# Stores of prepared weights ordered four steps behind the making of their low part, and an inverse square root spread over more steps

## The chip, the cores and the metric

The kernel runs on one core of a Trainium2 chip. Its time is device microseconds (us) for one execution. The kernel before took 1690.93 us (median of 3 runs, 1688.75 to 1692.35). One execution was profiled; its trace gives the rows below.

## The reference

Three layers, one behind the other, all with float32 results:

```python
# attention without softmax: batch 8, 8 heads, 576 positions, head size 64
kv  = einsum('bhsd,bhse->bhde', k, v)
out = einsum('bhsd,bhde->bhse', q, kv)
x   = out / sqrt(mean(out * out, -1) + 1e-6) * g_norm      # -> [4608, 512]
# layer 1, 512 -> 1536 -> 512
xn  = x / sqrt(mean(x * x, -1) + 1e-6) * rms_g
x   = (silu(xn @ w_gate) * (xn @ w_val)) @ w_out
# layer 2, 512 -> 2048 -> 512
h   = maximum(x @ w_in, 0)
out = (h * h) @ w_out2
```

The weights come as 64-bit floats.

## The kernel before, in words

**Tiling.** The 4608 rows are nine blocks of 512. They go through TensorE in stages: layer 1 on blocks 0 and 1 (stage 0), on block 2 (stage 1), then on pairs of blocks, then layer 2 in the same way. Every number that is multiplied is the sum of a high part (what TensorE's fast float32 form keeps) and a low part (the rest); a product takes three passes, high by high, low weight by high, high by low. Pairs of blocks, from stage 2 on, use a scheme of seven block products instead of eight, which needs sums and differences of quarters of the weights.

**Tick.** Six matmuls of 128x512 are one product, called here a product or a tick. After each, `tick()` advances the counter `now[0]` and emits what is due: work put off by `after`, the attention of the coming blocks (`chain`), and steps of the preparation of weights (`prep_step`). All instructions stand in the order in which the Python code emits them (a manual schedule); each engine works its own list off in that order, and SP (the queue that issues every DMA) too. A wait at the head of a list holds everything behind it.

**Preparation of a unit.** A unit is a 128x1024 piece of a weight matrix, named by letter and number (g0, v0, g1, v1, ... for gate and value, o for the first output matrix, i and p for layer 2). Its steps have fixed times: load (L131), three steps that turn 64-bit floats into 32-bit ones (`bits_1` on ScalarE, L139; `bits_2` and `bits_3` on VectorE, L143, L144, L150), the high part (`hi`, ScalarE, L180), the low part (`lo`, VectorE, L183), and a store of both to DRAM (`put`, SP, L192). Units of kind "all" then make the second half, the sums for the seven products, and have a second `hi`, `lo` and `put`. Steps of all units wait in one queue, `prep_q`, in the order of their times. `prep_step(False)`, which `tick` calls, leaves the step at the head of the queue for later while its `landed` says no. Where a weight is wanted that is not ready, `w_direct` (stage 0) and `w_fetch` (later stages) take steps from the queue at once, without asking `landed`.

**Weights in stage 0.** While weights are still being made, the products read the prepared tiles `ws` directly, g0 in products 0 to 3, v0 in 4 to 7, g1 in 8 to 11, v1 in 12 to 15, g2 in 16 to 19, v2 in 20 to 23. The high part is read by a product's first two matmuls, the low part by the next two. From stage 1 on a tile `wt` is fetched from DRAM into a ring of five. Fetching begins near the end of stage 0, and only when `prep_q` is empty:

```python
                    if first[0] and nb == 1 and n >= len(seq) - 3 and not prep_q:
                        streams[0] = True
```

**Attention.** For each block of 512 rows: four times an `o_mm` (TensorE), then `att_g` (L433, VectorE), squares on ScalarE (L442, L446) that overwrite the bank, and sums (L451); then at step u `att_m`, at u+1 the inverse square root by three Newton rounds (`att_r`, L470 to L481), at u+2 and u+3 the four products `att_y` (L493), and from u+9 the transposes (`x1_T`, L500, TensorE), which read all four. Block 1 (the `direct` one) has shorter times and is transposed into SBUF in stage 0 (`x_hi` L521, `x_lo` L525).

**What frees TensorE's banks.** In stages with seven products VectorE adds (L686) an accumulator to a copy; the product that writes this bank next waits for the addition.

Of the kernel before, what the change touches and what calls it, by code (L numbers as in the profile page):

```python
# [11 lines left out]
F32 = mybir.dt.float32  # L12
# [23 lines left out]
W_RING = 5  # L36
N_SUMS = 5
LAND = 6


@with_exitstack
def attn_moe_moe(
# [14 lines left out]
    nc = tc.nc  # L57
# [50 lines left out]
    def prep_unit(key, kind, raws, plains, outs, ahead=7):  # L108

        m, f = key  # L110
        src, place = w_src[m]
        pair, e = pair_of(key)
        if pair not in wd:
            wd[pair] = [dram.tile([128, 4, 2, 2, 256], F32, name=f"wd_{m}{f}_{h}") for h in range(2)]
        st = {}

        def plain_tile():

            at = next(plains)
            if len(at) == 2:  # L120
                t = at[0].tile([128, 2, 2, 512], F32, tag=at[1], name="wpl")
                st["s"], st["w"] = t[:, 0], t[:, 1]
            else:
                st["s"] = at[0].tile([128, 2, 512], F32, tag=at[1], name="wps")
                st["w"] = at[2].tile([128, 2, 512], F32, tag=at[3], name="wpw")

        def load():
            pool, tag = next(raws)
            st["t"] = now[0]
            st["r"] = pool.tile([128, 2, 512, 2], I32, tag=tag, name="wraw")  # L130
            nc.sync.dma_start(  # L131
                out=st["r"].rearrange("p u n w -> p (u n w)"), in_=src[f].rearrange("p u n -> p (u n)").bitcast(I32)
            )

        def bits_1():
            plain_tile()
            nc.scalar.activation(out=st["s"], in_=st["r"][:, :, :, 1].bitcast(F32), func=AF.Copy, scale=2.0**-112)  # L139

        def bits_2():
            hf, w = st["s"].bitcast(I32), st["w"].bitcast(I32)
            nc.vector.tensor_scalar(out=w, in0=hf, scalar1=-(2**31), scalar2=None, op0=ALU.bitwise_and)  # L143
            nc.vector.scalar_tensor_tensor(  # L144
                out=w, in0=st.pop("r")[:, :, :, 0], scalar=29, in1=w, op0=ALU.logical_shift_right, op1=ALU.bitwise_or
            )

        def bits_3():
            hf, w = st["s"].bitcast(I32), st["w"].bitcast(I32)
            nc.vector.scalar_tensor_tensor(  # L150
                out=w, in0=hf, scalar=3, in1=w, op0=ALU.logical_shift_left, op1=ALU.bitwise_or
            )

        def words_in():
            plain_tile()
            st["t"] = now[0]
            nc.sync.dma_start(out=st["w"], in_=wfd[key])

        def words_out():
            wfd[key] = dram.tile([128, 2, 512], F32, name=f"wf_{m}{f}")  # L160
            nc.sync.dma_start(out=wfd[key], in_=st["w"])

        def quarters(x):
            return x.rearrange("p u (h n) -> p (u h) n", h=2)

        def op(b, x, y, alu):
            of = {b: quarters(st["w"])[:, i] for b, (_, i) in place.items()}
            of |= {b: quarters(st["s"])[:, i] for b, (_, i) in PLACE_S.items()}
            nc.vector.tensor_tensor(out=of[b], in0=of[x], in1=of[y], op=alu)

        def hi(h):
            outs.rotate(-1)
            pool, tag = outs[-1]
            st["tag", h] = tag
            if kind in ("blocks", "words"):
                in_use[tag_of((pool, tag))] = key
            if pool is hop:
                hop_n[0] += 1
            st[h] = pool.tile([128, 4, 2, 256], F32R, tag=tag, name="ws")
            nc.scalar.activation(out=st[h][:, :, 0, :], in_=quarters(st["sw"[1 - h]]), func=AF.Copy)  # L180

        def lo(h):
            nc.vector.tensor_tensor(  # L183
                out=st[h][:, :, 1, :],
                in0=quarters(st["sw"[1 - h]]),
                in1=st[h][:, :, 0, :].bitcast(F32),
                op=ALU.subtract,
            )
            direct[key, h] = st[h]

        def put(h):
            nc.sync.dma_start(out=wd[pair][h][:, :, e], in_=st.pop(h).bitcast(F32))  # L192
            if not first[0] or h:
                put_at[st["tag", h]] = now[0]
            prepped.add((key, h))

        def sums():
            op("S1", "21", "22", ALU.add)
            op("S3", "11", "21", ALU.subtract)

        def hi_0():
            hi(0)

        def hi_1():
            hi(1)

        def sums_1():
            sums()

        def late(t):  # L210
            return now[0] - t >= LAND

        hi_0.ready = lambda: tag_of(outs[0]) not in in_use
        hi_0.landed = hi_1.landed = lambda: late(put_at.get(outs[0][1], -LAND))
        bits_1.landed = lambda: first[0] or late(st["t"])
        if kind == "sums":
            sums_1.landed = lambda: late(st["t"])
        head = [(-ahead, load), (-1 if kind == "all" else 1, bits_1), (2, bits_2), (3, bits_3), (4, hi_0), (5, lambda: lo(0))]
        tail = [
            (5, sums_1),  # L220
            (6, lambda: op("S2", "S1", "11", ALU.subtract)),
            (7, lambda: op("S4", "12", "S2", ALU.subtract)),
            (9, hi_1),
            (10, lambda: lo(1)),
            (13, lambda: put(1)),
        ]
        if kind == "all":
            return head + [(10, lambda: put(0))] + tail
        if kind == "blocks":
            return head + [(10, lambda: put(0))]  # L230
        if kind == "words":
            return head + [(8, words_out), (10, lambda: put(0))]
        return [(-2, words_in)] + tail

    in_use, put_at, hop_n = {}, {}, [0]
# [226 lines left out]
        nc.vector.tensor_scalar(out=z, in0=z, scalar1=1.0 / DM, scalar2=EPS, op0=ALU.mult, op1=ALU.add)  # L462
        m_t[j] = m

    def att_r(j):

        m = m_t.pop(j)
        a = small.tile([128, NS + NQ], F32, tag="a", name="a")
        r = small.tile([128, NS + NQ], F32, tag="r", name="r")
        nc.vector.tensor_scalar(  # L470
            out=a.bitcast(I32), in0=m.bitcast(I32), scalar1=1, scalar2=None, op0=ALU.logical_shift_right
        )
        nc.vector.tensor_scalar(
            out=r.bitcast(I32), in0=a.bitcast(I32), scalar1=-1, scalar2=MAGIC, op0=ALU.mult, op1=ALU.add
        )
        for _ in range(3):
            nc.vector.scalar_tensor_tensor(out=a, in0=r, scalar=-0.5, in1=r, op0=ALU.mult, op1=ALU.mult)
            nc.vector.tensor_tensor(out=a, in0=a, in1=m, op=ALU.mult)
            nc.vector.scalar_tensor_tensor(out=r, in0=a, scalar=1.5, in1=r, op0=ALU.add, op1=ALU.mult)
        rc = r[:, :NS].rearrange("p (c h) -> p c h", h=H)  # L480
        nc.vector.tensor_tensor(  # L481
            out=rc,
            in0=rc,
            in1=r[:, NS:].rearrange("p (c o) -> p c o", o=1).to_broadcast([128, NQ, H]),
            op=ALU.mult,
        )
        r_t[j] = r
# [54 lines left out]
    def o_events(j, t, gap, first_t, t_gap, direct=False):  # L542

        for c in range(NQ):
            i, u = j * NQ + c, t + gap * c
            if not direct:
                at(u, lambda i=i: (o_mm(i), q_load()))
            elif c:
                at(u, lambda i=i, c=c: (o_mm(i), q_load() if c == 1 else None))
            at(u + 1, lambda i=i: att_g(i))  # L550
            s = u if direct else u + 1
            at(s + 1, lambda i=i: att_sq(i))
            at(s + 2, lambda i=i: att_sum(i, 0))
            at(s + 3 - direct, lambda i=i: att_sg(i))
            at(s + 4 - direct, lambda i=i: att_sum(i, 1))
        u = t + gap * (NQ - 1) + (4 if direct else 6)
        at(u, lambda: att_m(j))
        at(u + 1, lambda: att_r(j))
        for c in range(NQ):
            at(u + 2 + c // 2, lambda c=c: att_y(j, c, nc.vector))  # L560
        for c in range(KC):
            v = first_t + t_gap * c
            if direct:
                at(v, lambda c=c: x1_T(j, c, tag="AB"[c % 2]))
                at(v + 1, lambda c=c: (x_hi(j, c), x_lo(j, c)))
            else:
                at(v, lambda c=c: x1_T(j, c))
                at(v + 1, lambda c=c: x1_out(j, c))
# [63 lines left out]
    def at(t, fn):  # L632
        seq_n[0] += 1
        insort(chain, (t, seq_n[0], fn))
# [370 lines left out]
    with tc.manual_schedule():  # L1005
# [68 lines left out]
        idle = psum.tile([128, 512], F32, tag="b5", name="idle")  # L1074
        keep(8)
        att_m(0)
        att_r(0)
        for c in range(NQ):
            att_y(0, c, nc.vector)
        prep_step()  # L1080
# [95 lines left out]
```

## Time and profile before

| what | before |
|---|---|
| median of 3 runs (lowest, highest) | 1690.93 us (1688.75, 1692.35) |
| the profiled execution | 1691.47 us, its span 1689.7 us |
| TensorE (PE) busy | 1656.5 us, 98% of the span |
| VectorE (DVE) busy | 1099.0 us, 65% |
| ScalarE (ACT) busy | 665.3 us, 39% |
| DMA of queue q1 | 441.54 MB, 77.1% of 16 engines' span |
| mean granted TensorE clock | 0.992 |

PE is TensorE's matmuls, PEld its weight loads. A row of the timeline gives start, length, engine, line, operation, tiles, and in brackets the idle time ahead of it with what ended it. The DMA's landing is the time at which the last of its data has arrived.

### The profile page before, as it was taken

To read this page: it belongs to the slowest core of one execution; us is meant where nothing else is said; L and a number is where in the kernel's file an instruction comes from. 1 tells how busy PE (TensorE), PEld (TensorE's weight loads), DVE (VectorE), ACT (ScalarE), POOL (GpSimd) and SP (SyncE) were. 2 spreads that over 40 slices of the span, in tenths; PEclk is the share of its full clock that TensorE was granted. 3 is DMA by queue.
4 is the path that set the end of the run, shared out by engine and by line. 5 is a ranking of instruction groups with operands and counts; after the bars stand their busy time and mean duration, and the time that the engine had idled before them with its cause. 6 is when DMAs were issued, how large, how long until landed. Compare 5 with 4: busy or idle time off the path is not lost.

```text
span 1689.7 us, 21279 instructions
## 1 busy us (share of the span) xinstructions
PE 1656.5 (98%) x8060; PEld 1361.2 (81%) x8060; DVE 1099.0 (65%) x1500; ACT 665.3 (39%) x908; POOL 0.7 (0%) x6
## 2 busy tenths in 40 slices
PE   8899999999999999999999999999999999999998
PEld 7688888788888887878888888878887887888887
DVE  6866685766885669653985347864884587468431
ACT  4332443244444444442543323533353345335331
POOL 0000000000000000000000000000000000000000
PEclk8999999999999999999999999999999999999999
DMA  9875689998998898787998866767676657766674
GB/s 327 270 285 222 235 279 350 367 341 291 374 319 279 272 334 312 263 316 248 347 356 281 280 212 194 239 200 217 195 241 201 212 193 238 212 206 217 194 226 142
DMA packets 146725, 442.89 MB, mean 262 GB/s; under 512 B 14016, under 2 KB 14016, under 8 KB 142272
## 3 DMA queue, kind: packets, MB, share of 16 engines
q1 hardware_dynamic: 146624, 441.54, 77.1%
q8 instruction: 64, 1.05, 0.2%
q14 instruction: 37, 0.30, 0.0%
HBM read 343.97 MB, written 97.52 MB: 261 GB/s over the span
## 4 chain that ended last, share of the span: by engine, by line
PE 82%; DVE 9%; DMA 6%; ACT 2%; issue 1%; SPq 0%; DVEq 0%; ACTq 0%
PE c L671 46%; PE acc L891 17%; PE a L926 9%; PE e L926 3%; PE d L926 3%; DVE ho L578 2%; PE ops L416 1%; DMA wt<-wd_o 1%; DMA wd_p<-ws 1%; DVE xo L578 1%; PE kvps L376 1%; PE ot L983 1%; DMA wt<-wd_g 1%; DVE ws L183 1%; DMA kvraw<-in_k_dram 1%
## 5 line engine op out<-in xcount | busy, mean ns | idle before, releaser
L671 PE MATMUL c<-xo,wt 128*128 128x512 f32 x3336 | 782.1, 392 | 6.7 <-DVE hr L686 4.2
L671 PEld LDWEIGHTS c<-xo,wt 128*128 128x128 f32 x3336 | 621.3, 188 | 136.8 <-DVE hr L686 5.5
L578 DVE TENSOR_TENSOR ho<-hr,ho 128x1024 fp32r<-128x1024 f32 x174 | 212.4, 1222 | 121.9 <-ACT ho L577 121.9
L891 PE MATMUL acc<-ho,wt 128*128 128x512 f32 x1200 | 278.4, 392 | 3.5 <-DMA wt<-wd_o 3.5
L891 PEld LDWEIGHTS acc<-ho,wt 128*128 128x128 f32 x1200 | 225.3, 189 | 51.7 <-DMA wt<-wd_o 4.7
L577 ACT ACTIVATE ho<-hr 128x1024 fp32r<-128x1024 f32 x174 | 183.7, 1058 | 171.8 <-PE acc L891 63.6
L686 DVE TENSOR_TENSOR c<-c,s 128x512 f32<-128x512 f32 x150 | 103.3, 688 | 163.2 <-PE c L671 155.7
L682 ACT ACTIVATE s<-c 128x512 f32<-128x512 f32 x204 | 120.9, 596 | 165.0 <-PE c L671 164.2
L926 PE MATMUL a<-ho,wt 128*128 128x512 f32 x768 | 178.7, 390 | 2.5 <-DVE ho L578 2.5
L926 PEld LDWEIGHTS a<-ho,wt 128*128 128x128 f32 x768 | 143.4, 188 | 35.2 <-DVE ho L578 5.6
L671 PE MATMUL c<-xo,ws 128*128 128x512 f32 x576 | 141.7, 400 | 7.9 <-ACT ws L180 4.9
L671 PEld LDWEIGHTS c<-xo,ws 128*128 128x128 f32 x576 | 107.1, 190 | 32.8 <-ACT ws L180 5.7
L686 DVE TENSOR_TENSOR hr<-c,s 128x512 f32<-128x512 f32 x54 | 37.1, 687 | 82.7 <-PE c L671 81.9
L926 PE MATMUL e<-ho,wt 128*128 128x512 f32 x384 | 88.3, 389 | 0.0
L743 DVE TENSOR_TENSOR hr<-c,hr 128x512 f32<-128x512 f32 x108 | 73.9, 686 | 19.0 <-PE c L671 17.5
L926 PEld LDWEIGHTS e<-ho,wt 128*128 128x128 f32 x384 | 72.1, 188 | 15.0
L738 ACT ACTIVATE r<-c 128x512 f32<-128x512 f32 x48 | 28.7, 598 | 137.0 <-PE c L671 137.0
L581 DVE TENSOR_TENSOR hr<-hr 128x1024 f32<-128x1024 f32 x64 | 78.2, 1222 | 1.1
L691 ACT ACTIVATE sg<-hr 128x512 f32<-128x512 f32 x54 | 34.1, 632 | 111.1 <-DVE hr L686 111.1
L578 DVE TENSOR_TENSOR xo<-xr,xo 128x1024 fp32r<-128x1024 f32 x53 | 64.2, 1219 | 16.4 <-ACT xo L577 16.2
L739 DVE TENSOR_TENSOR hr<-c,r 128x512 f32<-128x512 f32 x48 | 33.2, 692 | 61.2 <-ACT r L738 61.1
L691 ACT ACTIVATE sg<-c 128x512 f32<-128x512 f32 x54 | 32.1, 595 | 99.8 <-PE c L671 99.6
(79 smaller groups left out, 1281.7 us busy)
## 6 DMA issues: line engine op xcount, KB each, us to landing
wt<-wd_g SPq DMA_DIRECT2D x150, 512.0 KB, 6.4
wt<-wd_i SPq DMA_DIRECT2D x128, 512.0 KB, 4.1
wt<-wd_p SPq DMA_DIRECT2D x128, 512.0 KB, 4.7
wt<-wd_o SPq DMA_DIRECT2D x84, 512.0 KB, 4.5
wd_g<-ws SPq DMA_DIRECT2D x24, 1024.0 KB, 9.5
wd_i<-ws SPq DMA_DIRECT2D x16, 1024.0 KB, 7.6
wd_p<-ws SPq DMA_DIRECT2D x16, 1024.0 KB, 8.0
wraw<-in_wo_dram SPq DMA_DIRECT2D x14, 1024.0 KB, 7.5
```

Source lines behind the costliest of these rows:

```text
L577: nc.scalar.activation(out=dst[:, 0], in_=src, func=AF.Copy)
L578: eng.tensor_tensor(out=dst[:, 1], in0=src, in1=dst[:, 0].bitcast(F32), op=ALU.subtract)
L581: eng.tensor_tensor(out=o, in0=x, in1=y, op=ALU.subtract)
L671: nc.tensor.matmul(ps, lhsT=w[:, a, kc * 128:(kc + 1) * 128], rhs=x[:, b, kc, :], start=(start and n == 0 and kc == 0), stop=(n == 2 and k ...
L682: nc.scalar.activation(out=t, in_=ps, func=AF.Copy)
L686: nc.vector.tensor_tensor(out=o, in0=ps, in1=t, op=ALU.add)
L691: nc.scalar.activation(out=sg, in_=c, func=AF.Sigmoid)
L738: nc.scalar.activation(out=t, in_=c, func=AF.Relu)
L739: after(1, lambda: nc.vector.tensor_tensor(out=hr, in0=c, in1=t, op=ALU.mult))
L743: after(2, lambda: nc.vector.tensor_tensor(out=hr, in0=c, in1=hr, op=ALU.mult))
L891: nc.tensor.matmul(acc[c], lhsT=wt[:, a, (c % 2) * 128:(c % 2 + 1) * 128], rhs=x[:, b, e, :], start=(n == 0 and e == 0 and a + b == 0), st ...
L926: nc.tensor.matmul(ps, lhsT=w[e][:, a, d * 128:(d + 1) * 128], rhs=x[:, b, e, :], start=(i in (1, 2, 5) and q == 0 and e == 0 and a + b == 0),
```

## The change

The store of a half gets a `landed` of its own: it stays in the queue until four ticks after that half's low part was emitted. As `prep_q` is one queue, the steps behind it stay too. The root of a block that is not `direct` is emitted in three ticks (u+1, u+2, u+3), and its four products in the four ticks u+4 to u+7 instead of two each at u+2 and u+3. The transposes stay at u+9. No arithmetic is added or taken away.

```diff
+MADE = 4
@@ prep_unit
                 op=ALU.subtract,
             )
+            st["lo", h] = now[0]
             direct[key, h] = st[h]
...
+        def put_0():
+            put(0)
+
+        def put_1():
+            put(1)
+
+        put_0.landed = lambda: now[0] - st["lo", 0] >= MADE
+        put_1.landed = lambda: now[0] - st["lo", 1] >= MADE
...
-            (13, lambda: put(1)),
+            (13, put_1),
         ]
         if kind == "all":
-            return head + [(10, lambda: put(0))] + tail
+            return head + [(10, put_0)] + tail
...
-    def att_r(j):
-
-        m = m_t.pop(j)
...
-        for _ in range(3):
-            nc.vector.scalar_tensor_tensor(out=a, in0=r, scalar=-0.5, in1=r, op0=ALU.mult, op1=ALU.mult)
-            nc.vector.tensor_tensor(out=a, in0=a, in1=m, op=ALU.mult)
-            nc.vector.scalar_tensor_tensor(out=r, in0=a, scalar=1.5, in1=r, op0=ALU.add, op1=ALU.mult)
+    def att_r(j, n):
+
+        m = m_t[j]
+        if n == 0:
...
+            r_t[j] = r, a
+        r, a = r_t[j]
+        nc.vector.scalar_tensor_tensor(out=a, in0=r, scalar=-0.5, in1=r, op0=ALU.mult, op1=ALU.mult)
+        nc.vector.tensor_tensor(out=a, in0=a, in1=m, op=ALU.mult)
+        nc.vector.scalar_tensor_tensor(out=r, in0=a, scalar=1.5, in1=r, op0=ALU.add, op1=ALU.mult)
+        if n < 2:
+            return
+        m_t.pop(j)
...
         at(u, lambda: att_m(j))
-        at(u + 1, lambda: att_r(j))
+        for n in range(3):
+            at(u + 1 + (0 if direct else n), lambda n=n: att_r(j, n))
         for c in range(NQ):
-            at(u + 2 + c // 2, lambda c=c: att_y(j, c, nc.vector))
+            at(u + (2 + c // 2 if direct else 4 + c), lambda c=c: att_y(j, c, nc.vector))
```

TensorE's list is the same in both kernels. Lines of the changed kernel have higher numbers than those of the kernel before (L183 is L184 there, L192 is L194, L335 is L345). Three places follow.

**First place: VectorE near the start of stage 0**, products 1 to 6, where v0 and g1 are prepared. `wpw<-wps,wpw` is `bits_3`, `ws<-wpw,ws` a low part, `y`, `ss` and `hr` belong to the attention of block 1 and to the gate. Before:

```order
L433 TENSOR_TENSOR y<-ops,gn_sb 128x512
L451 TENSOR_REDUCE ss_482<-ops 128x8
L150 SCALAR_TENSOR_TENSOR wpw<-wps,wpw 128x1024
L451 TENSOR_REDUCE ss_483<-ops 128x8
L692 TENSOR_TENSOR hr<-c,sg 128x512
L433 TENSOR_TENSOR y<-ops,gn_sb 128x512
L183 TENSOR_TENSOR ws<-wpw,ws 128x4x256
L451 TENSOR_REDUCE ss_482<-ops 128x8
```

And in the changed kernel:

```order
L443 TENSOR_TENSOR y<-ops,gn_sb 128x512
L461 TENSOR_REDUCE ss_482<-ops 128x8
L461 TENSOR_REDUCE ss_483<-ops 128x8
L708 TENSOR_TENSOR hr<-c,sg 128x512
L443 TENSOR_TENSOR y<-ops,gn_sb 128x512
L461 TENSOR_REDUCE ss_482<-ops 128x8
L151 SCALAR_TENSOR_TENSOR wpw<-wps,wpw 128x1024
L184 TENSOR_TENSOR ws<-wpw,ws 128x4x256
```

v0's `bits_3` moved behind four attention instructions and stands directly ahead of its low part; the store of g0, which cannot go before tick 4, had held the queue. The later units of stage 0 up to v2 are each one tick later in the same way; from product 33 on the two lists agree again until product 110.

**Second place: SP at the end of stage 0**, products 137 to 144. `wd_g_1_...<-ws` are stores of weights' sums, `wt<-wd_g_0_122` the fetches of stage 1's first weights, `kvraw` loads wait until the matmuls of an earlier tile are done. Before:

```order
L192 DMA wd_g_1_125<-ws 512x1x512
L515 DMA x1d_104<-x_2208 128x512
L192 DMA wd_g_1_127<-ws 512x1x512
L335 DMA wt<-wd_g_0_122 128x1024 x2
L364 DMA kvraw<-in_k_dram 128x512
L365 DMA kvraw<-in_v_dram 128x512
L515 DMA x1d_104<-x_2258 128x512
L335 DMA wt<-wd_g_0_122 128x1024 x2
```

And in the changed kernel:

```order
L194 DMA wd_g_1_125<-ws 512x1x512
L374 DMA kvraw<-in_k_dram 128x512
L375 DMA kvraw<-in_v_dram 128x512
L530 DMA x1d_104<-x_2254 128x512
L194 DMA wd_g_1_127<-ws 512x1x512
L345 DMA wt<-wd_g_0_122 128x1024 x4
L345 DMA wt<-wd_g_0_124 128x1024
L993 DMA x2d_111<-o 128x512 x2
```

The last store of this phase moved behind the two `kvraw` loads and one more store, from tick 140 to 144, and all fetches of weights stand behind it.

**Third place: SP in the last stage of layer 1**, products 445 to 454, where a unit of layer 2 (p) is stored in two halves between fetches of layer 1's output weights (`wt<-wd_o`). Before:

```order
L618 DMA xr<-x1d_108 128x1024 x2
L192 DMA wd_p_0_148<-ws 512x1x512
L192 DMA wd_p_1_149<-ws 512x1x512
L335 DMA wt<-wd_o_0_138 128x1024
L335 DMA wt<-wd_o_0_134 128x1024 x3
```

And in the changed kernel:

```order
L634 DMA xr<-x1d_108 128x1024 x2
L194 DMA wd_p_0_148<-ws 512x1x512
L345 DMA wt<-wd_o_0_138 128x1024
L345 DMA wt<-wd_o_0_134 128x1024
L194 DMA wd_p_1_149<-ws 512x1x512
L345 DMA wt<-wd_o_0_134 128x1024 x2
```

The second store moved behind two fetches. The same pair of lists stands once more in layer 2's second stage, at products 579 to 584.

## Rows read from the trace of the kernel before

**Rows 1.** The page: busy time of each engine

```profile
PE 1656.5 (98%) x8060; PEld 1361.2 (81%) x8060; DVE 1099.0 (65%) x1500; ACT 665.3 (39%) x908; POOL 0.7 (0%) x6
```

**Rows 2.** Waits of TensorE's matmuls: total us, times, longest us

```profile
PE c L671 <- DVE hr L686: 4.2, 3, 3.8
PE acc L891 <- DMA wt<-wd_o: 3.5, 2, 2.7
...
PE c L671 <- DMA wt<-wd_g: 2.4, 3, 1.2
```

**Rows 3.** Timeline of TensorE, 36 to 84 us, stage 0

```profile
66.88 1.22 PE L671 MATMUL c<-xo,ws 128*128 128x512 f32 x2 [3.14 <-ACT ws L180]
69.94 4.11 PE L671 MATMUL c<-xo,ws 128*128 128x512 f32 x10 [1.83 <-DVE ws L183]
...
77.91 1.64 PE L671 MATMUL c<-xo,ws 128*128 128x512 f32 x6
```

**Rows 4.** Timeline of all engines, 37 to 42 us

```profile
37.73 1.22 DVE L150 SCALAR_TENSOR_TENSOR wpw<-wps,wpw 128x1024 int32<-128x1024 int32 x1
...
38.98 1.06 ACT L180 ACTIVATE ws<-wpw 128x1024 fp32r<-128x1024 f32 x1
...
40.06 0.68 DVE L433 TENSOR_TENSOR y<-ops,gn_sb 128x512 f32<-128x512 f32 x1
40.66 1.22 DVE L183 TENSOR_TENSOR ws<-wpw,ws 128x1024 fp32r<-128x1024 f32 x1
40.78 0.58 ACT L442 ACTIVATE ops<-ops 128x512 f32<-128x512 f32 x1 [0.73 <-DVE y L433]
```

**Rows 5.** Timeline of all engines, 77 to 81 us

```profile
77.75 0.60 ACT L691 ACTIVATE sg<-c 128x512 f32<-128x512 f32 x1 [0.53 <-PE c L671]
...
78.25 1.26 ACT L521 ACTIVATE xo<-xps,rg_sb 128x512 fp32r<-128x512 f32 x2
78.96 0.75 DVE L525 SCALAR_TENSOR_TENSOR xo<-xps,rg_sb,xo 128x512 fp32r<-128x512 f32 x1 [0.84 <-ACT xo L521]
```

**Rows 6.** Timeline of SP, 258 to 275 us, end of stage 0

```profile
263.12 2.60 SPq L335 DMA_DIRECT2D wt<-wd_g  x2
267.88 0.33 SPq L364 DMA_DIRECT2D kvraw<-in_k_dram  x1
...
269.42 1.56 SPq L335 DMA_DIRECT2D wt<-wd_g  x3
```

**Rows 7.** Timeline of TensorE, 266 to 276 us

```profile
272.47 3.79 PE L671 MATMUL c<-xo,wt 128*128 128x512 f32 x16
```

**Rows 8.** Instructions of tile wt, 263 to 265.8 us: landings

```profile
DMA to landing us min/median/max: 7.7/7.7/7.8
```

**Rows 9.** Chain of waits, 730 to 756 us: start, length, what

```profile
736.84 0.51 SPq L192
...
737.45 10.29 DMA wt<-wd_o
...
747.78 8.27 PE acc L891 x28
```

**Rows 10.** Instructions of tile wd_p, 730 to 760 us: the two stores' landings

```profile
DMA to landing us min/median/max: 9.6/10.0/10.4
```

**Rows 11.** Windows: length, busy times (instructions), granted clock, DMA share, GB/s

```profile
670.60:674.10 3.50, 3.48 (x8) 2.80 (x9) 3.40 (x5) 0.94 (x2) 0.00 (x0) 0.51 0.97 313
749.10:752.60 3.50, 3.50 (x10) 2.72 (x9) 0.00 (x0) 1.03 (x2) 0.00 (x0) 0.51 0.95 382
```

**Rows 12.** Timeline of all engines, 650 to 676 us

```profile
664.47 1.29 DVE L493 TENSOR_TENSOR y<-y,r 128x512 f32<-128x512 f32 x2
...
669.88 0.68 DVE L686 TENSOR_TENSOR hr<-c,s 128x512 f32<-128x512 f32 x1
...
670.62 4.59 PE L671 MATMUL c<-xo,wt 128*128 128x512 f32 x12 [3.80 <-DVE hr L686]
...
675.05 0.60 PE L500 MATMUL xps<-ident,y 128*128 128x128 f32 x4
```

More of the change, by code (lines that the diff above doesn't have):

```diff
@@ L224, in prep_unit @@
             (10, lambda: lo(1)),
-            (13, lambda: put(1)),
+            (13, put_1),
         ]
         if kind == "all":
-            return head + [(10, lambda: put(0))] + tail
+            return head + [(10, put_0)] + tail
         if kind == "blocks":
-            return head + [(10, lambda: put(0))]
+            return head + [(10, put_0)]
         if kind == "words":
-            return head + [(8, words_out), (10, lambda: put(0))]
+            return head + [(8, words_out), (10, put_0)]
         return [(-2, words_in)] + tail
@@ L463, in att_m @@
         m_t[j] = m
-    def att_r(j):
-        m = m_t.pop(j)
[L468 to L475, printed above, removed]
-        for _ in range(3):
-            nc.vector.scalar_tensor_tensor(out=a, in0=r, scalar=-0.5, in1=r, op0=ALU.mult, op1=ALU.mult)
-            nc.vector.tensor_tensor(out=a, in0=a, in1=m, op=ALU.mult)
-            nc.vector.scalar_tensor_tensor(out=r, in0=a, scalar=1.5, in1=r, op0=ALU.add, op1=ALU.mult)
+    def att_r(j, n):
+        m = m_t[j]
+        if n == 0:
+            a = small.tile([128, NS + NQ], F32, tag="a", name="a")
+            r = small.tile([128, NS + NQ], F32, tag="r", name="r")
+            nc.vector.tensor_scalar(
+                out=a.bitcast(I32), in0=m.bitcast(I32), scalar1=1, scalar2=None, op0=ALU.logical_shift_right
+            )
+            nc.vector.tensor_scalar(
+                out=r.bitcast(I32), in0=a.bitcast(I32), scalar1=-1, scalar2=MAGIC, op0=ALU.mult, op1=ALU.add
+            )
+            r_t[j] = r, a
[6 more added lines that the diff above has]
+        m_t.pop(j)
         rc = r[:, :NS].rearrange("p (c h) -> p c h", h=H)
@@ L1076, in attn_moe_moe @@
         att_m(0)
-        att_r(0)
+        for n in range(3):
+            att_r(0, n)
         for c in range(NQ):
```

## The prediction

> **What bounds the kernel now.** I began with the busy times: PE is busy 98% of the span [rows 1], so only its few idle stretches can be won, and any new one is paid in full. Then the waits of PE's matmuls [rows 2], and a timeline of stage 0 [rows 3], show where these stretches are. Three kinds matter. In stage 0 PE waits for weights that are still being made: at 66.88 us it had idled 3.14 us for a high part, at 69.94 another 1.83 us for a low part. In later stages it waited once 3.8 us for an addition on VectorE, at 670.62 [rows 2, 12], and twice for a fetched weight of `wd_o`, 2.7 us and, of the 3.5 in all, 0.8 us [rows 2]. Last, the granted clock: after the waits of 3.8 and of 2.7 us it stood at half, 1.2 GHz, for some 3.4 us [rows 11], in which PE does half its work: 1.7 us lost each time, beside the wait itself. A wait of this length so costs 5.5 or 4.4 us. (One product is six matmuls; 16 take 3.79 us, less the 0.39 of the last one's own length, over 15 steps: 0.227 us each, 1.36 us a product [rows 7].)
>
> Who made PE wait at 747.78 is told by the chain of waits [rows 9]: a store on SP waited for a low part until 736.84, the fetch behind it was issued at 737.45 and took 10.29 us to land. The two stores ahead took 9.6 to 10.4 us [rows 10]: 736.84 + 9.6 = 746.4, and the fetch landed at 747.74, 1.3 us after it. Data arrive here in the order of issue, one transfer behind the other, 1.3 us for 512 KB, so 2.6 for a store of 1 MB.
>
> **The change part by part.** No instruction is added; everything is a matter of order, so each term is a wait won or a wait made.
>
> *Stage 0, v0 to g2.* Before, v0's `bits_3` (L150, from 37.73) and its high part (38.98) ran while VectorE and ScalarE did attention, and the low part ended at 40.66 + 1.22 = 41.88 [rows 4]. Now `bits_3` stands behind the next `y` and the sum that waits for the square of it (first place of the change). Without L150 ahead of it `y` starts at most 0.4 us sooner, since the gate's product ahead of it waits for ScalarE: 39.7. Then `y` 0.7, square 0.6, the sum's step 0.6, L150 1.22, L180 1.06, L183 1.22, each waiting for the one before it: 45.1 or 45.2 us. That is 3.3 us later, and PE wants v0 at product 4, where it hardly waited before. Behind this, g1, v1 and g2 have the same instructions ahead of their low parts as before, so only the idle time of VectorE counts that I find in the new order and not in the old (mainly L183 directly behind its own L150, with L180 between). Followed down to g2, L183 ends at about 72.8 instead of 69.9, and product 17 ends 2.9 us later. Bounds: 0, if other work fills the idle time after all, and 4.
>
> *Stage 0, v2.* Its low part now stands behind the second `x_lo`, which waits for the second `x_hi`, which stands on ScalarE behind a gate that waits for product 19; and v2 is wanted by product 20. From 77.75 on: gate 0.5, `x_hi` 0.7, `x_lo` 0.75, low part 1.22 (steps from [rows 5], L183 from [rows 4]) makes 81.0. PE began product 20 at 77.91 [rows 3] and has two matmuls, 0.45 us, to do without the low part: a wait of 2.6 us. A wait of 0.2 that follows there now goes: +2.4. This wait is a little shorter than the 2.7 after which the clock fell, so I add 1.0 of 1.7 for the clock. Bounds for both: 0 and 5.
>
> *End of stage 0.* Fetches start only when the queue of preparation is empty. Its last step is a store, now four ticks later, so all fetches move behind the `kvraw` loads (second place). Before, two fetches were issued from 263.12, landed 7.7 us later, 270.8 and 272.1 [rows 6, 8], and PE took the first at 272.47 without a wait [rows 7]. Now SP is held at `kvraw` until 267.88, needs 1.54 us for these loads and a store, to 269.42 [rows 6], and 0.5 for the 1 MB store [rows 9]: the first fetch is issued at 269.9. Ahead of its data lie three transfers of 256 KB and the store: by 1.3 us for 512 KB, 1.9 + 2.6 us, and 1.3 for its own. If the first data arrive as late after 267.88 as a lightly loaded transfer (an estimate: the second fetch's 7.7 us less 1.3 of the first and 2.6 of the store ahead of both, 3.8 in all, its own data included, so 2.5 before them), it lands at 267.9 + 2.5 + 5.8 = 276.2, say 276.5: PE waits 4.0 us, and the clock falls, 1.7 more: +5.7. Lower bound: 269.9 + 3.8 = 273.7, with nothing ahead, a wait of 1.2 and no fall of the clock; upper 5.0 + 1.7.
>
> *End of layer 1's last stage.* The second store moves behind two fetches (third place). The first fetch then lands right behind the first store (746.4 - 2.6 = 743.8): 745.1. PE wanted it at 747.78 - 2.7 = 745.1. The wait goes, and the clock with it: -2.6 - 1.7 = -4.3. The third fetch lands as before, since the same bytes are ahead of it; it is next to be late, with about 0.4 us to spare. Its like in layer 2: -0.8. Bounds for both: 0 and -5.2.
>
> *The root in more steps.* It matters where VectorE is behind, at 670. Before, from 664.47 to 669.88 four `y` (0.6 us a step), a low part (1.1) and `bits_2` (the other 1.9 of these 5.4 us) stood ahead of the addition that PE waited for, which ended at 669.88 + 0.68 = 670.56 [rows 12]. The `y` and `bits_2`, 4.3 us, now come after it; a low part (1.1) and idle time that the older order filled come back. I get 667.4: the wait shrinks from 3.8 to 0.5. But the last `y` now stands behind six more instructions and three `y` of 0.6 us each: 673.4. The transposes, which read it, are due two products after the addition, 667.4 + 2.7 = 670.1, and wait 3.3 us. Before they began at 675.05 [rows 12], with the clock's loss in it; now at 673.4, with the loss still to come if the clock falls again: 0, between -1.6 and +0.5. In the other blocks VectorE is less far behind.
>
> *The fetches in stage 1* (2.4 us of waits for `wd_g` [rows 2]): a store changes places with one fetch, the next fetch takes the wait over; 0, between -2.4 and +1.
>
> Sum: +2.9 + 2.4 + 1.0 + 5.7 - 4.3 - 0.8 + 0 + 0 = +6.9 us against the profiled execution's 1691.47, so 1698.4; that execution lies 0.5 above the median of the runs, so 1698 for the median.
>
> **The rivals.** *Loads overtake stores* at the end of stage 0: then the first fetch lands at 273.7, PE waits 1.2 us and the clock stays: 5.7 becomes 1.2, and the time is 1693.5. For it: nothing in these rows shows a fetch behind a store on an otherwise idle queue; against it: at 747 the fetch did come behind both stores [rows 9, 10]. The Trainium skill, page "DMA: Bandwidth & Descriptors", section "Queues, rings and completion order", says that completion is not FIFO per issuing engine; by it the sum would be +2.4. The landings of rows 9 and 10 do not bear this out here.
>
> *The root's spread wins after all*: if VectorE is 3.3 us less behind at 670 than I follow it, both the addition and the transposes are in time, -3.8 - 1.7 = -5.5. The sum is then +1.4; the kernel becomes faster from the point at which the new waits in stage 0 stay under 7.2 of the 12.0 I count, for instance with no fall of the clock there (2.7) and the first fetch at its lower bound (2.8 less): 6.5 - 5.1 - 5.5 = -4.1, 1687. For it: 3.3 us is less than what moves at that place. Against: both must come together.
>
> *The clock falls more often*: with waits of 2 to 4 us at products 4, 8, 16 and 20 stage 0 may run much of its time at half clock; PE then becomes late itself. Three more falls of 1.7: 1703.5. For it: the falls in rows 11 after single waits. Against: while VectorE makes PE wait anyhow a slower PE costs nothing.
>
> **How the numbers follow.** The forecast, both start costs and the won store: 0.60, by itself 1695 to 1702. Overtaking, or one start cost missing: 0.16, about 1693.5. The root's win with small start costs: 0.14, 1685 to 1692. More falls of the clock: 0.10. Less than 0.2%, 3.4 us, is what a measurement of this kernel can't tell from no change, so 1687.5 to 1694.3 is the same: 0.10 of the second case, 0.04 of the third and 0.01 of the first, 0.15; faster is the rest of the third, 0.10; slower 0.75. The range, 1689 to 1704, leaves out most of the third case's faster part and half of the fourth.
>
> **What would show it.** In the new trace PE should wait some 3 us for `ws` at about 44 us, where it did not, and 2.5 us at product 20; the first matmul on `wt` should wait about 4 us for `wt<-wd_g` behind a store; the wait for `wd_o` at 747 should be gone; the addition at 670 should be early and the transposes there wait for `y`. Wrong it is if the first low parts are ready in time for product 4, if the first fetch lands before PE asks, or if neither addition nor transpose waits at 670.

## The result and the profile after

The changed kernel takes 1702.75 us (median of 4 runs, 1700.10 to 1704.51), 1.0062 times the kernel before, with a 95% interval of 1.0050 to 1.0074: it is slower, by some 10.5 us (8.5 to 12.5). The forecast of 1698 had the sign and most of the places; it was some 4 to 5 us short. The profiled execution took 1702.82 us; its span of 1701.0 is 11.3 us longer than that of the kernel before.

The busy times, to be read beside [rows 1], say that no work was added: all is waiting and clock.

```profile
PE 1661.3 (98%) x8060; PEld 1363.8 (80%) x8060; DVE 1099.8 (65%) x1500; ACT 666.2 (39%) x908; POOL 0.7 (0%) x6
```

The waits of TensorE's matmuls (total us, times, longest us) show what took which place. Against [rows 2], the wait of 3.8 us for `hr` and both waits for `wd_o` are nearly gone; in their stead stand 5.9 us for `wd_g` (before: 2.4), 4.6 for `y`, and some 4.6 more than before for `ws`. The changed kernel, then the two rows for `ws` before:

```profile
PE c L687 <- ACT ws L181: 6.8, 4, 3.2
PE c L687 <- DMA wt<-wd_g: 5.9, 2, 5.3
PE c L687 <- DVE ws L184: 5.6, 5, 2.3
...
PE xps L515 <- DVE y L508: 4.6, 6, 1.5
...
PE acc L907 <- DMA wt<-wd_o: 0.5, 1, 0.5
...
PE c L687 <- DVE hr L702: 0.4, 1, 0.4
```
```profile
PE c L671 <- ACT ws L180: 4.9, 2, 3.1
...
PE c L671 <- DVE ws L183: 2.9, 3, 1.8
```

Since TensorE's list is the same in both kernels, the most useful reading is the start of the same matmul in both traces. The column "gained or lost" of this table (my subtraction) is a budget by place, and its sum is the difference of the ends. It compares one execution with one other.

| up to the start of product | before, us | after, us | late by | gained or lost on the way | forecast |
|---|---|---|---|---|---|
| 0 | 34.70 | 34.89 | 0.2 | +0.2 | 0 |
| 18 (v0 to g2) | 74.24 | 77.54 | 3.3 | +3.1 | +2.9 |
| 22 (v2) | 81.65 | 88.56 | 6.9 | +3.6 | +2.4 + 1.0 |
| 140 (end of stage 0) | 265.70 | 274.13 | 8.4 | +1.5 | 0 |
| 152 (first fetch) | 285.06 | 301.86 | 16.8 | +8.4 | +5.7 |
| 260 (stage 1) | 455.68 | 471.22 | 15.5 | -1.3 | 0 |
| 345 | 584.07 | 601.45 | 17.4 | +1.8 | 0 |
| 410 (the place at 670) | 684.16 | 701.65 | 17.5 | +0.1 | 0 |
| 462 (the place at 747) | 760.42 | 773.32 | 12.9 | -4.6 | -4.3 |
| 600 (930, layer 2) | 950.15 | 961.50 | 11.4 | -1.6 | -0.8 |
| 1120 | 1677.14 | 1688.58 | 11.4 | +0.1 | 0 |

**Start of stage 0.** The timeline of all engines, to be read beside [rows 4]: `y`, then `bits_3` (L151), the high part (L181) and the low part (L184) of v0, and TensorE's two waits for them.

```profile
39.71 0.68 DVE L443 TENSOR_TENSOR y<-ops,gn_sb 128x512 f32<-128x512 f32 x1
41.64 1.22 DVE L151 SCALAR_TENSOR_TENSOR wpw<-wps,wpw 128x1024 int32<-128x1024 int32 x1
42.89 1.06 ACT L181 ACTIVATE ws<-wpw 128x1024 fp32r<-128x1024 f32 x1 [0.23 <-DVE wpw L151]
43.98 1.22 DVE L184 TENSOR_TENSOR ws<-wpw,ws 128x1024 fp32r<-128x1024 f32 x1 [1.12 <-ACT ws L181]
44.00 0.73 PE L687 MATMUL c<-xo,ws 128*128 128x512 f32 x2 [2.46 <-ACT ws L181]
45.26 1.20 PE L687 MATMUL c<-xo,ws 128*128 128x512 f32 x4 [0.53 <-DVE ws L184]
```

The low part ends at 43.98 + 1.22 = 45.20 us, as forecast to the tenth (45.1 or 45.2), and PE waits 3.0 us at product 4. Further on TensorE stays 3 to 4 us late, with waits for g1, v1 and g2 that are split otherwise between their high and low parts.

**Product 20.** The rows around 82 us, to be read beside [rows 5]: the second `x_hi` on ScalarE, the second `x_lo` (L540), then v2's low part, and PE.

```profile
81.53 0.68 ACT L536 ACTIVATE xo<-xps,rg_sb 128x512 fp32r<-128x512 f32 x1
82.24 0.75 DVE L540 SCALAR_TENSOR_TENSOR xo<-xps,rg_sb,xo 128x512 fp32r<-128x512 f32 x1 [2.89 <-ACT xo L536]
82.91 1.22 DVE L184 TENSOR_TENSOR ws<-wpw,ws 128x1024 fp32r<-128x1024 f32 x1
84.18 2.08 PE L687 MATMUL c<-xo,ws 128*128 128x512 f32 x4 [2.28 <-DVE ws L184]
```

**The first fetch.** SP's list at the end of stage 0, to be read beside [rows 6]; then the landings of that store and of the first fetch (us from issue, the smaller is the store's), and the first matmuls on `wt`.

```profile
276.31 0.33 SPq L374 DMA_DIRECT2D kvraw<-in_k_dram  x1
...
277.55 0.33 SPq L530 DMA_DIRECT2D x1d<-x  x1
277.98 0.52 SPq L194 DMA_DIRECT2D wd_g<-ws  x1
278.55 4.31 SPq L345 DMA_DIRECT2D wt<-wd_g  x5
```
```profile
DMA to landing us min/median/max: 6.3/7.0/7.8
```
```profile
278.04 3.02 PE L907 MATMUL acc<-ho,ws 128*128 128x512 f32 x12
286.37 7.12 PE L687 MATMUL c<-xo,wt 128*128 128x512 f32 x18 [5.31 <-DMA wt<-wd_g]
```

The order of landing is that of the list: the store at 277.98 + 6.3 = 284.3, the fetch at 278.55 + 7.8 = 286.3, and PE starts with it. While these two landed, the DMA engines were busy all the time (share 1.01) but moved 315 GB/s, against 400 in the window behind them (below):

```profile
281.00:286.30 5.30, 0.06 (x1) 0.00 (x0) 0.00 (x0) 0.60 (x1) 0.00 (x0) 0.92 1.01 315
```

**The clock.** Windows behind three waits that are new or have moved (2.28, 5.31, and 0.96 with 1.48 us), and one at the place of 747 (length, busy times, granted clock, DMA share, GB/s). Half clock, 1.2 GHz, stands in all of the first three:

```profile
84.20:87.50 3.30, 3.30 (x10) 2.73 (x11) 3.01 (x4) 0.36 (x1) 0.00 (x0) 0.50 0.22 83
286.40:292.30 5.90, 5.90 (x14) 4.66 (x15) 0.00 (x0) 0.35 (x1) 0.00 (x0) 0.50 1.03 400
691.70:695.00 3.30, 3.30 (x10) 2.53 (x9) 3.23 (x5) 0.72 (x1) 0.00 (x0) 0.50 0.39 141
762.00:766.00 4.00, 4.00 (x19) 3.34 (x18) 0.30 (x1) 1.83 (x4) 0.00 (x0) 1.00 1.04 415
```

The last of these is the place of 747 in [rows 11]: full clock now, and TensorE ran through it without a wait (one row of its timeline, 90 matmuls):

```profile
754.74 20.56 PE L907 MATMUL acc<-ho,wt 128*128 128x512 f32 x90
```

Half clock does not stand behind every wait, nor always as long. Behind the new waits at product 4 (2.46 and 0.53 us) the clock stayed full in this execution. Behind g2's wait of 3.21 us at 70.85 it stood at half from 70.5 to 77.2 us, much as in the kernel before. The window behind product 4, changed kernel, then that of g2 before:

```profile
44.00:47.00 3.00, 2.47 (x13) 1.86 (x14) 3.00 (x4) 0.98 (x1) 0.00 (x0) 1.00 0.89 348
```
```profile
66.50:73.30 6.80, 4.59 (x10) 3.19 (x11) 6.76 (x9) 1.37 (x2) 0.00 (x0) 0.50 0.76 262
```

**The place at 670**, now at 685, to be read beside [rows 12]. The addition (L702) comes in time and PE does not wait for it; the transposes (L515) wait for the third and the fourth `y` (L508), which stand among additions and gates:

```profile
684.44 0.68 DVE L702 TENSOR_TENSOR hr<-c,s 128x512 f32<-128x512 f32 x1
...
688.64 0.69 DVE L508 TENSOR_TENSOR y<-y,r 128x512 f32<-128x512 f32 x1
...
689.38 0.33 PE L515 MATMUL xps<-ident,y 128*128 128x128 f32 x1 [0.96 <-DVE y L508]
...
690.44 0.69 DVE L508 TENSOR_TENSOR y<-y,r 128x512 f32<-128x512 f32 x1
...
691.18 0.33 PE L515 MATMUL xps<-ident,y 128*128 128x128 f32 x1 [1.48 <-DVE y L508]
```

### The profile page after: what moved, and what is told of

Its sections match the earlier page's. It is cut to its first block, busy times and chain, and to the rows that moved or that the text cites. A ratio compares the mean times of both kernels' runs of the same rounds, so it can differ in the third digit from the quotient of the medians.

```text
span 1701.0 us, 21280 instructions
## 1 busy us (share of the span) xinstructions
PE 1661.3 (98%) x8060; PEld 1363.8 (80%) x8060; DVE 1099.8 (65%) x1500; ACT 666.2 (39%) x908; POOL 0.7 (0%) x6
## 4 chain that ended last, share of the span: by engine, by line
PE 81%; DVE 10%; DMA 5%; ACT 2%; issue 1%; SPq 0%; DVEq 0%; ACTq 0%
PE c L687 48%; PE acc L907 15%; PE a L942 9%; PE e L942 3%; PE d L942 3%; DMA kvraw<-in_v_dram 2%; DMA xr<-x1d 2%; DVE xo L594 1%; DVE ho L594 1%; PE kvps L386 1%; PE ops L426 1%; DVE xr L597 1%; DMA wt<-wd_g 1%; PE ot L999 1%; PE xps L515 1%
## 5 line engine op out<-in xcount | busy, mean ns | idle before, releaser
L702 DVE TENSOR_TENSOR c<-c,s 128x512 f32<-128x512 f32 x150 | 103.3, 689 | 165.3 <-PE c L687 155.6
L702 DVE TENSOR_TENSOR hr<-c,s 128x512 f32<-128x512 f32 x54 | 37.2, 688 | 81.3 <-PE c L687 81.2
```

What stands on the lines that cost most here:

```text
L702: nc.vector.tensor_tensor(out=o, in0=ps, in1=t, op=ALU.add)
```

## The experiments

Times are given against the kernel before, run on the same chip: the ratio with its 95% interval, and us as the ratio times 1691. Two theories stood against each other at first. P: the cost sits where a held store delays weights, place by place. R: the spread root sets VectorE back, and the rest follows.

**The two halves of the change.** Held stores alone:

```diff
-            at(u + 1 + (0 if direct else n), lambda n=n: att_r(j, n))
+            at(u + 1, lambda n=n: att_r(j, n))
...
-            at(u + (2 + c // 2 if direct else 4 + c), lambda c=c: att_y(j, c, nc.vector))
+            at(u + 2 + c // 2, lambda c=c: att_y(j, c, nc.vector))
```

> The held stores alone, the root and its four products as in the kernel before. Theory P (the cost sits at the places where a held store delays weights, and adds up place by place: start of stage 0 +6.8, first fetch of stage 1 +8.2, fetches in stage 1 -1.1, 747 us -4.1, 870 and 930 us -1.5): 1691.5 + 8.3 = 1699.8 us, the transposes' waits for y (4.6 us in the changed kernel) gone, VectorE's addition at about 685 us late again by some 3.8. Theory R (the spread root puts VectorE behind, and the late weights follow from that): about 1691, PE waits for ws and wd_g as in the kernel before.

Measured: 1.0053 (1.0040 to 1.0066), +9.0 us. Its waits begin like those of the changed kernel (for the low parts 6.0 us), with 0.3 us for `y` in place of 4.6:

```profile
PE c L687 <- DMA wt<-wd_g: 6.8, 3, 5.4
PE c L687 <- ACT ws L181: 6.5, 3, 3.2
```

P holds and R falls. One detail was off: TensorE waited 2.3 us for the addition at 688 us, not 3.8, so the held stores by themselves already help it.

The spread root alone:

```diff
-MADE = 4
+MADE = 0
```

> The spread root and products alone, every store as in the kernel before (MADE is 0). Theory P: no wait at products 4, 20 and 144; transposes wait for y, +1.6 at the end of stage 0, +1.1, +0.8 and +1.2 up to 680 us; the addition at 670 us early, -5.3, the transposes behind it late, +3.8; in sum +3.2, so 1694.7 us. Theory R: about 1702, with the long waits of stage 0 still there.

Measured: 1.0006 (0.9997 to 1.0014), +1.0 us (-0.5 to +2.4); expected was +3.2. No wait at products 4, 20 and 144, as P says. But the small waits that I had put down to the root do not come: of the transposes only those at the old place of 670 wait for `y`, and the wait for `wd_o` is there again. The timeline of TensorE at both places (this profiled execution took 1698.86 us where the median of the 12 runs is 1695.23, so its places count here, not its sum):

```profile
670.90 3.02 PE L687 MATMUL c<-xo,wt 128*128 128x512 f32 x12 [1.13 <-DVE hr L702]
...
676.23 0.33 PE L515 MATMUL xps<-ident,y 128*128 128x128 f32 x1 [2.09 <-DVE y L508]
678.03 0.33 PE L515 MATMUL xps<-ident,y 128*128 128x128 f32 x1 [1.47 <-DVE y L508]
```
```profile
753.26 7.12 PE L907 MATMUL acc<-ho,wt 128*128 128x512 f32 x23 [3.77 <-DMA wt<-wd_o]
```

The two halves add up to +10.0 us, the whole is +10.5.

**Stage 0 without held stores.**

```diff
-        put_0.landed = lambda: now[0] - st["lo", 0] >= MADE
+        put_0.landed = lambda: first[0] or now[0] - st["lo", 0] >= MADE
```

(and `put_1` in the same way; `first[0]` is true while stage 0 runs).

> The changed kernel, but stores wait for nothing while stage 0 runs. Theory P: 6.8 and 8.2 us go, the gains at 747 and 930 us stay: 1702.75 - 15.0 = 1687.7 us, no wait over 0.3 us for wt<-wd_g at product 144. Rival S (slack: PE's late start only moves waits, what stage 0 wins back is waited for again at the fetches or at the root): 1695 or more.

Measured: 0.9975 (0.9964 to 0.9986), -4.2 us: faster than both kernels. Nothing is passed on: at product 152 it is 0.75 us behind the kernel before (285.82 against 285.06 us), and the place of 747 gives its 4.6 us as in the table. Rival S falls. The waits of 0.6 and 0.5 us at the transposes around 260 us, which the forecast lacked, are gone too, so they belong to the stores held in stage 0.

**Held only at the start of stage 0.**

```diff
-        put_0.landed = lambda: now[0] - st["lo", 0] >= MADE
+        put_0.landed = lambda: first[0] and now[0] > 30 or now[0] - st["lo", 0] >= MADE
```

(and `put_1` in the same way).

> The changed kernel, but from tick 31 of stage 0 to its end stores wait for nothing, so only the first 30 products keep the held stores. Theory P: the wait for the first fetch (5.3 us, 8.2 with the clock) goes, the start's +6.8 stays: 1702.75 - 8.2 = 1694.5 us, 6.8 above the kernel that is free in all of stage 0. Rival S2 (the first fetch is late because the start of stage 0 put everything late, not because of the last store): it still waits 4 us or more, 1702.

Measured: 0.9999 (0.9991 to 1.0008), -0.2 us; expected was +3. The wait for the first fetch is gone, so rival S2 falls: the last store made it. But the start costs only 4.0 us here (-0.2 less -4.2), not 6.8. In its trace PE waits for v2 as long as in the changed kernel, yet the clock stays full behind it, and the wait ahead of it, for g2's high part, is 1.8 us in place of 3.2. PE's timeline, then the window that in the changed kernel stood at half:

```profile
70.85 0.73 PE L687 MATMUL c<-xo,ws 128*128 128x512 f32 x2 [1.79 <-ACT ws L181]
...
83.50 1.20 PE L687 MATMUL c<-xo,ws 128*128 128x512 f32 x4 [2.28 <-DVE ws L184]
```
```profile
83.50:86.80 3.30, 3.30 (x16) 2.75 (x17) 3.27 (x5) 0.69 (x1) 0.00 (x0) 1.00 0.36 133
```

So behind one and the same wait of 2.28 us the clock may fall or not; what decides it in one execution stays open, and with it some 2 to 3 us of the start's cost. Other traces vary here too. With held stores alone and in this run TensorE waits 2.68 and 0.53 us at product 4, and the granted clock behind it is 0.50 (45.2 to 48.5 and 45.0 to 48.3 us), where it stayed full in the changed kernel.

**Is the clock a price of its own?** Matmuls that change no result are put ahead of products 20 and 144: they write the bank that the product then starts anew.

```diff
     def product(ps, w, x, start):
+        for _ in range({20: 10, 144: 22}.get(now[0], 0)):
+            nc.tensor.matmul(
+                ps, lhsT=x[:, 0, 0, :128], rhs=x[:, 0, 0, :], start=True, stop=False, skip_group_check=True
+            )
```

> The changed kernel, with TensorE kept at work ahead of its two long waits: the first matmul of product 20 is preceded by 10 and that of product 144 by 22 more matmuls into the same bank, which the first true one starts anew (10 x 0.227 = 2.3 us, 22 x 0.227 = 5.0 us, less than the waits of 2.28 and 5.31 us). Theory K (half clock follows an idle wait, and costs 1.2 us behind product 20 and 2.8 us behind product 144, on top of the waits): the weights come as late as before, but the granted clock stays at 1.0 after both places; -4.0, so 0.9976 of the changed kernel, some 6.5 us over the kernel before. Rival L (PE loses this time since its next weights come late, too, or the clock would fall at these places anyway): the time of the changed kernel, 10.5 to 11.5 us over the kernel before.

Measured: 1.0037 (1.0025 to 1.0049), +6.3 us, where +6.5 was expected and the changed kernel has +10.5. The weights come as late as before, but PE does not stand idle ahead of them (L686 are the added matmuls), and the windows that were at half are at full clock:

```profile
82.14 2.56 PE L686 MATMUL c<-xo 128*128 128x512 f32 x10
84.54 1.78 PE L691 MATMUL c<-xo,ws 128*128 128x512 f32 x6
```
```profile
279.82 5.15 PE L686 MATMUL c<-xo 128*128 128x512 f32 x22
285.25 4.37 PE L691 MATMUL c<-xo,wt 128*128 128x512 f32 x18 [0.27 <-DMA wt<-wd_g]
```
```profile
286.00:291.90 5.90, 5.90 (x31) 5.01 (x31) 1.38 (x2) 1.16 (x2) 0.00 (x0) 1.00 1.05 382
84.50:87.80 3.30, 3.30 (x17) 2.42 (x16) 3.27 (x5) 0.96 (x2) 0.00 (x0) 1.00 0.41 157
```

Theory K holds: 31 matmuls (8 of them the small ones of the attention) now pass in the 5.9 us in which 14 did. The late data are one price, the clock behind an idle wait is another, and the second can be had back without the first. Product 144 is the clear case, since behind product 20 the clock can stay full without help, as the run before shows.

**The fetch ahead of the last store.**

```diff
-                    if first[0] and nb == 1 and n >= len(seq) - 3 and not prep_q:
+                    if first[0] and nb == 1 and n >= len(seq) - 3 and len(prep_q) <= 1:
```

> The changed kernel, but the fetches of stage 1 may begin while one step, the last store, is still in the queue of preparation; that store stays four ticks late. Theory F (the fetch is late because it stands behind kvraw loads and the last store in SP's list): two fetches are issued some 13 us earlier, land before PE asks, the wait of 5.3 us and the half clock behind it go: -8.2, some 3 us over the kernel before. Rival D (the DMA engines are full at this place, 1.0 busy, so whatever goes first delays the rest): the next fetches or the transposes wait instead, a wait of 3 us or more in the ten products after 144, and the time falls by less than 4 us.

Measured: 1.0005 (0.9994 to 1.0016), +0.8 us (-1.0 to +2.7), so about 9.7 below the changed kernel; expected was 8.2. The store is as late as before (278.59), two fetches go at 271.08, and PE takes the first without a wait or a half clock:

```profile
271.08 1.91 SPq L345 DMA_DIRECT2D wt<-wd_g  x2
...
278.59 0.52 SPq L194 DMA_DIRECT2D wd_g<-ws  x1
```
```profile
281.81 4.24 PE L687 MATMUL c<-xo,wt 128*128 128x512 f32 x18
```

No wait of 3 us follows in the next ten products, as rival D had it; the next for `wd_g` is 0.6 us. So it is the order on SP that costs here: the same bytes are moved, and with two fetches ahead of the store no long wait is left.

**The root, once the stores are put right.** Stores free in stage 0, and the transposes two ticks later:

```diff
-                    o_events(j, t0, 5, t0 + 30, 4)
+                    o_events(j, t0, 5, t0 + 32, 4)
```

> The changed kernel with stores free in stage 0, and the transposes of every block from the third on two ticks later (t0 + 32 in place of t0 + 30). Theory Y (the transposes wait for the last y, which the spread root made four ticks later): the waits at about 494 (1.0) and 673 to 675 us (2.4, and 1.3 of half clock behind them) go, -4.7 against the kernel that is only free in stage 0, some 8.5 us under the kernel before. Rival X (the transposes' place is set by what reads them: x1d is stored later, and the loads xr<-x1d or VectorE are late in their place): no faster than the kernel that is only free in stage 0, or slower.

Measured: 0.9949 (0.9929 to 0.9968), -8.6 us: faster than both kernels, and the best of all that were run. No transpose waits for `y` any more. Part of the gain is given back at the same place: TensorE's timeline shows two new waits for ScalarE, which stood 4.95 us behind a high part that waited for `bits_3` (ScalarE's row, below).

```profile
676.50 3.01 PE L687 MATMUL c<-xo,wt 128*128 128x512 f32 x12 [1.63 <-ACT s L698]
680.90 0.66 PE L515 MATMUL xps<-ident,y 128*128 128x128 f32 x4 [1.39 <-ACT x L523]
```
```profile
674.90 1.06 ACT L181 ACTIVATE ws<-wpl 128x1024 fp32r<-128x1024 f32 x1 [4.95 <-DVE wpl L151]
```

The clock stays full there, so theory Y holds. The two new waits, for ScalarE, are not those that rival X named.

Stores free in stage 0 as above, the root as in the kernel before:

```diff
+        put_0.landed = lambda: first[0] or now[0] - st["lo", 0] >= MADE
...
+            at(u + 1, lambda n=n: att_r(j, n))
...
+            at(u + 2 + c // 2, lambda c=c: att_y(j, c, nc.vector))
```

> Stores free in stage 0 and held after it, the root and its products as in the kernel before: against the kernel that is free in stage 0 it has the old root alone. By the runs so far (held stores alone wait 2.3 us for the addition at 688 us, the changed kernel none there but 2.4 and the half clock for y): theory N (the root's spread as it stands is worth nothing here, since what it wins at the addition it gives back at the transposes): the same within 1.5 us, about 4 us under the kernel before. Rival W (the spread is a net win at this place): 2 to 4 us slower than the kernel that is free in stage 0.

Measured: 0.9976 (0.9963 to 0.9988), -4.1 us, the same as with the spread root (-4.2). Theory N holds: the spread as the change makes it is worth nothing, and with later transposes some 4.4 us (-8.6 against -4.2; the two intervals just meet). Later transposes with the old root were not run, so that the 4.4 us need the spread is not shown. What speaks for it: with the old root TensorE waits 2.25 us for the addition at 672.7 us, which does not hang on the transposes, and there not for `y`.

## Why the prediction was right, and where it was short

- *v0 to g2, +2.9*: right, +3.1; the low part of v0 ended at the forecast tenth.
- *v2, +2.4 and +1.0 for the clock*: right, +3.6, a wait of 2.28 us and a fall of the clock from 84.2 to 87.5. That these two came so close is in part luck. The same order stands at the start of stage 0 in three more runs. Counted from its own product 0, the changed kernel is 6.7 us late at product 24, where 6.3 was forecast. Held stores alone are 8.6 late, the run with the fetch ahead of the last store 8.5, the one held only at the start 5.4. In all three the clock fell behind product 4 as well, which it did not in the changed kernel nor in the run with the added matmuls; in the last it did not fall behind v2.
- *End of stage 0, +5.7*: the mechanism was right (the fetch behind `kvraw` and the last store), shown by two experiments that took it away in different ways; the term was mis-sized, +8.4. Two steps of it failed. The first is "2.5 + 5.8" us from SP's release to the landing: it took 10.0 (276.31 to 286.33), and PE waited 5.3 us, not 4.0. Up to the landing of the store `x1d` at 280.94 the sum held (4.6 us, forecast 4.4). Then the store of 1 MB took 3.3 us, not 2.6, and the fetch 2.1, not 1.3. The price of 1.3 us for 512 KB had been read at 747 us. At the end of stage 0 the trace of the kernel before had 2.9 us for such a store (landings at 266.0 and 268.9) and 2.0 for the fetch behind it (270.9). The second is "1.7 more" for the clock: TensorE worked 5.9 us at half clock here, not 3.4, and lost 2.9. That half clock can stand longer than 3.4 us was to be seen at 66.5 us in the kernel before (6.8).
- *747 us, -4.3, and 930 us, -0.8*: right, -4.6 and -1.6; the second includes a wait of 0.2 us for `hr` at 870 us that went. In the other runs with held stores new waits of 0.5 to 0.8 us, mostly for an addition (L702) at product 529, take part of the second back, so its size is that of one execution.
- *The root at 670, 0*: right in sum, +0.1, and in both its parts: the addition in time, 2.4 us of waits for `y` (3.3 in the forecast), and the clock's fall that moved behind them.
- *Stage 1's fetches, 0 (-2.4 to +1)*: -1.3; this wait was partly won.
- *Small waits, not forecast*: +1.5 at the end of stage 0, +1.8 from product 260 to 345. The step that failed is the sentence "In the other blocks VectorE is less far behind": with the stores held, the steps of preparation behind them stand elsewhere among the attention, and the transposes at 258, 264, 509 and 600 us wait 0.3 to 1.0 us each (at 264 for ScalarE's `x`, else for `y`). With the spread root alone they don't; held stores with the old root lose about as much in these stretches, partly at other instructions. So it is the stores that do it.

The rivals: that loads overtake stores does not happen. In both traces each of the 860 transfers that SP issued lands behind the one issued ahead of it. By the rule of the Trainium skill that stood beside it (page "DMA: Bandwidth & Descriptors", section "Queues, rings and completion order") the fetch might have come first; the rule allows that, the trace does not show it. That the root's spread wins by itself fell with its own experiment. "The clock falls more often" gave a number near the measured one, 1703.5, but for another reason: in this execution the fall at 749 went, those at 84 and 286 came, and the one at 670 only moved; the time beyond the forecast is longer transfers, a longer half clock at one place, and small waits. In three other executions its fall behind product 4 does come.

The clock fell behind idle waits of TensorE, as in [rows 11], though not behind all of them, and did not where the same waits were filled with matmuls. The Trainium skill, page "TensorE: Matmul & The Clock Gate", section "HAM oscillation — how this bites in real kernels", tells that a wait for data makes the clock fall, so that the work behind it starts slow. The trace agrees for the wait of 5.31 us (granted 0.50 behind it). It does not make a rule for the shorter ones: behind 2.28 us the clock fell in one kernel and not in another.

## What to carry to other kernels

When a step is held back in a queue that others share, list what stands behind it there: here a store that nobody reads soon held the steps that make the next weights, and all fetches. Hold back where the trace shows a fetch waiting behind a store (747 us: -4.6 us), and leave free where someone is waiting for what is queued behind (stage 0: 14.7 us between the changed kernel and the one that is free there). And when a chain of steps is spread over more time, move its reader by as much: here the spread was worth nothing until its transposes moved along, then some 4.4 us, with the control named above not run.

## What was not expected of the hardware

- Behind the longest wait (5.3 us) TensorE worked 5.9 us at half clock, behind those of 2.28 and of 0.96 with 1.48 us 3.3: this cost 2.9 us there and 1.6 to 1.7 here. A wait of 3.2 us had half clock for 6.7 us (70.5 to 77.2), so the length of the wait alone does not tell how long it stands.
- Matmuls whose results are thrown away, put into a wait, kept the granted clock at 1.00 and saved about 4 us of 1700, at two places.
- A store of 1 MB between loads took 3.3 us of the shared transfer time at the end of stage 0 (from the landing at 280.94 us of the store ahead of it to its own at 284.27) and 2.9 at the same place in the kernel before, not the 2.6 that two fetches of 512 KB take. At 744 to 746 us in the kernel before it took 2.5, so the price is one of the place.
